# One change in four places of a fused attention and mixture-of-experts kernel: fp16 gate, early comparisons, other PSUM banks, another order on VectorE

## The chip, the cores and the metric

The kernel runs on one core of a Trainium2 chip. The metric is the device time of one execution in microseconds; the time before is the median of 3 runs. Engines: TensorE (PE for products, PEld for loading weights), VectorE (DVE), ScalarE (ACT), GpSimd (POOL) and SyncE (SP), which issues most transfers.

## The reference

Attention over 8 batches, 8 heads, 576 positions of 64, in two parts that are added: one on means of 4 positions, one local with |i - j| < 4. Its result, as 4608 tokens of 512, goes through a mixture of 8 experts of capacity 576. Pairs of token and expert are taken greedily in the order of their logits, so the routing follows the exact order of the logits.

```python
out_up = np.repeat(sm_attn(q_d, k_d, v_d), 4, axis=2)      # q_d: means of 4 positions
attn = softmax(np.where(abs(i - j) < 4, scale * q @ k.T, -1e9))
x = (out_up + attn @ v).transpose(0, 2, 1, 3).reshape(4608, 512)
logits = x @ w_gate                                        # 4608 x 8
for idx in np.argsort(-logits.flatten()):
    tok, e = idx // 8, idx % 8
    if assigned[tok] < 0 and counts[e] < 576:
        assigned[tok] = e; counts[e] += 1
for e in range(8):
    m = assigned == e
    out[m] = np.maximum(x[m] @ w1[e], 0) @ w2[e]           # 512 -> 1024 -> 512
```

## The kernel before, in words

**Attention** works on 36 units of 128 tokens. Each unit has stages (`LOC`): scores of 4 windows into the one PSUM tile `s` (`loc_s`), then maximum and difference on VectorE (L439, L440), exponential on ScalarE, transposes (`loc_t`), products with v (`loc_v`) and the normalising on VectorE (L397 to L400). Then `log_a` adds the other part of attention, `log_t` transposes the unit's 128 x 512 result and ScalarE scales it by XS into `xt` (fp32), and `log_m` multiplies it with the gate's weights `wgf` (fp32) into logits, which VectorE copies to `lg`. All but the scores use the 6 banks `g` in turn. The order is written out by hand: a list of works, sorted by a due time in units; `after(n, f)` puts a work n TensorE pieces later. Between the units stand the transposes and products of the other part of attention, batch by batch, so units lie at uneven distances. After unit 25 and after unit 35 a generator `setup` is stepped through: it makes 16-bit keys, high `xh` and low `xl`, out of the logits.

**Routing** takes one expert at a time (`phase`). Every token stands for its best open expert; a search on the high key and then on the low key finds the threshold at which the first expert fills. `count` does a search in levels: 64, 32 and 32 thresholds. On each level VectorE compares keys with thresholds (L687), TensorE counts by products (L717), VectorE subtracts (L725), sets a flag (L728), a product spreads it (L730), a reduction finds the level's answer (L732). In the first phase the first level's comparisons are made in `first_compare` into tiles `cmp0` of a pool that takes over the attention's memory, and counts below the first level take two token tiles to a product (`n = 2`), in the others four. `emit` ranks the chosen tokens and makes their list `idx`; `self.done` is its last operation. Then follow updates of the routing's state (`gl` to `used`, L914 to L931).

**Experts.** `gather` fetches an expert's 576 tokens by `idx` with 5 indirect transfers on GpSimd's queue. For the first two experts `piece` transposes them on TensorE into banks `pX` (2 of them), ScalarE writes the high fp16 half (L1057), VectorE the low one (L1058). For later experts a DMA transposes. `split` turns weights into fp16 halves, `wh` on ScalarE (L1026) and `wl` on VectorE (L1028). `mlp` computes products high x high, high x low, low x high: first 8 blocks of the hidden layer into banks `pH` (two tiles of 2 banks), whose result leaves as halves `ht` (ScalarE L1105, VectorE L1108), then 5 parts of tokens into `pX` (L1121). Each part is scaled by ScalarE and sent with an indirect transfer.

A scheduler orders the experts' part by priority; `high_priority` raises it, `issue_after(ins)` puts what is issued inside behind `ins` on the engine of `ins`, `behind_` does so for two instructions. `in1` is called after each hidden block and holds weight pieces (for the first expert, those of its own second product; later, those of the next expert); `in2` after each part of the second product, where the second expert's rows are transposed (`GET0`: pieces 0 and 1 after part 3, the others after part 4). `BEHIND` puts the second routing's rank products behind the first expert's second product, and `TURN` sets the place of the later transposes of the first expert's rows.

Of the kernel before, what the change touches and what calls it, by code (L numbers as in the profile page):

```python
# [6 lines left out]
F32 = mybir.dt.float32  # L7
F16 = mybir.dt.float16
# [82 lines left out]
class Attention:  # L91
    def __init__(self, ctx, tc, q, k, v, wg, ident, identb, maskc, x_dram, up_dram, lg, big, more=()):
# [20 lines left out]
        self.wgf = cst.tile([128, 4, E], F32, name="wgf")  # L113
        for t, src in ((self.ident, ident), (identh, identb), (self.mask, maskc)) + tuple(more):
            nc.scalar.dma_start(t, src)
# [17 lines left out]
    def gate(self):  # L133
        nc = self.nc
        nc.scalar.mul(self.wgf, self.wgf, GS)
# [349 lines left out]
    def log_t(self, u):  # L485
# [5 lines left out]
        xt = self.xt[u] = self.wk.tile([128, 4, 128], F32, name="xt", bufs=TB)  # L491
        nc.scalar.activation(xt.rearrange("p c t -> p (c t)"), p.rearrange("p c t -> p (c t)"), AF.Copy, scale=XS)

    def log_m(self, u):
        nc = self.nc
        xt = self.xt.pop(u)
# [138 lines left out]
class Routing:  # L635
    def __init__(self, ctx, tc, lg, consts):
# [22 lines left out]
        self.cuts = []  # L659
# [24 lines left out]
    def compare(self, cmp, key, thr, a, b):  # L684
        w = min(SW, thr.shape[1])
        r = thr.shape[1] // w
        self.nc.vector.tensor_tensor(cmp[:, a:b].rearrange("p t (r j) -> p t r j", r=r),  # L687
                                     key[:, a:b, None, :w].to_broadcast([128, b - a, r, w]),
                                     thr.rearrange("p (r j) -> p r j", r=r)[:, None].to_broadcast([128, b - a, r, w]),
                                     op=OP.is_ge)  # L690

# [4 lines left out]
    def first_compare(self, key, cut):  # L696
        cmp = self.wk.tile([128, NT, LV[0][0]], BF, name="cmp0", bufs=2)
        for a, b in cut:
            self.compare(cmp, key, self.first, a, b)
        return cmp  # L700

    def count(self, oh, key, cmp, cap, full=None):
# [4 lines left out]
        for lv, (J, step) in enumerate(LV):  # L707
# [4 lines left out]
            n = 2 if self.cut is HALF else 128 // J  # L712
# [15 lines left out]
            nc.vector.tensor_tensor(fl[:J], cv[:J, :, 0], left[:J], op=OP.is_ge)  # L728
# [42 lines left out]
    def setup(self, a, b, first=False):  # L771
# [14 lines left out]
        if first:  # L786
            self.cuts += [(c, min(c + 18, b)) for c in range(a, b, 18)]
# [57 lines left out]
    def phase(self, last, first=False, known=None):  # L845
# [20 lines left out]
        if first:  # L866
            xh = self.v["xh"]
            early = self.first_compare(xh, self.cuts)
# [6 lines left out]
        if not first:  # L875
            early = self.first_compare(xh, WHOLE)
        H = self.count(oh, xh, early, lambda: self.cap)
        cmp0 = self.first_compare(xl, self.cut)
# [405 lines left out]
```

## Time and profile before

| | |
|---|---|
| median of 3 runs | 776.08 us (773.46 to 778.11) |
| profiled execution | 776.02 us, span 774.4 us |
| mean granted clock of TensorE | 0.941 |
| busy: TensorE, its loads, VectorE, ScalarE, GpSimd | 698.9, 498.9, 509.3, 331.1, 242.0 us |
| DMA | 124.98 MB, mean 161 GB/s |

The profile is that of one execution. Busy times overlap; a share of the span is a mean over stages with different limits. A clock of 1.00 is 2.4 GHz, one of 0.50 is 1.2 GHz. Rows of a time line are start, length, engine, line, operation, tiles and count; brackets hold the engine's idle time before the row and what ended it.

### The profile page before, as it was taken

What the parts mean: (1) busy time and instruction counts of PE and PEld (TensorE: products, weight loads), DVE (VectorE), ACT (ScalarE), POOL (GpSimd) and SP (SyncE); (2) the same over time, 40 slices, a digit from 0 to 9 for tenths busy, and PEclk for the clock granted to TensorE, in tenths of its full rate; (3) what the DMA queues carried; (4) which work ended last, traced back from release to release, by engine and by line L of the source; (5) the groups of instructions that cost most, each with busy time, mean ns of one, the idle gap of its engine ahead of it and who ended that gap; (6) DMA issues with size and microseconds to landing.
All of it is one profiled execution on the core that took longest, in us unless ns stands there. A gap on an engine that the chain in (4) does not pass through costs nothing.

```text
span 774.4 us, 20987 instructions
## 1 busy us (share of the span) xinstructions
PE 698.9 (90%) x8513; PEld 498.9 (64%) x8513; DVE 509.3 (66%) x1530; ACT 331.1 (43%) x635; POOL 242.0 (31%) x289
## 2 busy tenths in 40 slices
PE   7798999998999993589999999999999999999994
PEld 4677788887888893356466456356456465574752
DVE  5766576765676736877878989899979345271210
ACT  4546567673767430342523426135225244252210
POOL 4756264534537340300530413150230402201011
PEclk9789799997999985689999999999999999999998
DMA  9988889897988750522614566471673884605001
GB/s 261 215 230 212 236 225 256 235 231 237 240 206 216 177 165 11 185 95 91 210 41 147 171 145 219 90 279 36 191 211 109 118 283 95 199 1 102 22 28 34
DMA packets 148048, 124.98 MB, mean 161 GB/s; under 512 B 92144, under 2 KB 122352, under 8 KB 147952
## 3 DMA queue, kind: packets, MB, share of 16 engines
q1 hardware_dynamic: 140656, 102.12, 49.0%
q0 software_dynamic: 6432, 20.98, 9.0%
q8 instruction: 67, 1.10, 0.6%
q10 hardware_dynamic: 864, 0.55, 0.3%
q14 instruction: 29, 0.24, 0.1%
HBM read 95.30 MB, written 21.23 MB: 150 GB/s over the span
## 4 chain that ended last, share of the span: by engine, by line
PE 38%; issue 23%; DVE 23%; ACT 6%; DMA 4%; POOL 3%; SPq 1%; POOLq 0%; DVEq 0%; ACTq 0%
PE pH L1082 7%; DVE wl L1028 5%; PE g L499 4%; PE pX L1121 4%; PE g L472 4%; DMA nat<-in_k_dram 3%; PE g L289 3%; DVE cmp L687 3%; POOL out_dram L1130 2%; DVE ht L1108 2%; PE s L430 2%; PE g L450 2%; PE g L490 2%; PE g L366 2%; ACT pt L461 2%
## 5 line engine op out<-in xcount | busy, mean ns | idle before, releaser
L1082 PE MATMUL pH<-xt,wh 128*128 128x256 f16 (+1 forms) x1024 | 196.1, 288 | 7.8 <-DVE ht L1108 3.5
L1121 PE MATMUL pX<-wh,ht 128*128 128x512 f16 (+1 forms) x640 | 179.7, 384 | 2.3 <-DVE xt L1058 2.3
L1121 PEld LDWEIGHTS <-ht 128*128 128x128 f16 (+1 forms) x960 | 84.0, 101 | 100.6 <-issue 11.6
L1082 PE MATMUL pH<-xt,wl 128*128 128x320 f16 (+1 forms) x512 | 147.5, 288 | 0.0
L1130 POOL DMA_INDIRECT out_dram<-y,idx x40 | 47.3, 1181 | 248.6 <-ACT y L1127 226.6
L1082 PEld LDWEIGHTS <-wh 128*128 128x128 f16 x1024 | 98.7, 98 | 35.3 <-issue 7.3
L1121 PE MATMUL pX<-wl,ht 128*128 128x512 f16 (+1 forms) x320 | 119.2, 384 | 0.0
L1105 ACT ACTIVATE ht<-pH 128x512 f16<-128x512 f32 (+1 forms) x128 | 45.5, 408 | 128.7 <-PE pH L1082 128.7
L1028 DVE SCALAR_TENSOR_TENSOR wl<-nat,wh 128x512 f16<-128x512 f32 x128 | 84.8, 686 | 7.6 <-ACT wh L1026 5.2
L1127 ACT ACTIVATE y<-pX 128x512 f32<-128x512 f32 (+1 forms) x40 | 23.8, 594 | 130.9 <-PE pX L1121 83.5
L1108 DVE SCALAR_TENSOR_TENSOR ht<-pH,ht 128x512 f16<-128x512 f32 (+1 forms) x128 | 52.6, 451 | 34.1 <-ACT ht L1105 33.1
L1026 ACT ACTIVATE wh<-nat 128x1024 f16<-128x1024 f32 x64 | 66.8, 1057 | 4.7 <-DMA nat<-in_moe_w_dram 4.4
L1043 POOL DMA_INDIRECT xg<-x_dram,idx x40 | 47.8, 1195 | 57.7 <-DVE xs L1065 24.8
L1082 PEld LDWEIGHTS <-wl 128*128 128x128 f16 x512 | 50.3, 98 | 15.4 <-issue 3.2
L461 ACT COPY pt<-g 64x512 f32<-64x512 f32 x72 | 41.7, 579 | 37.1 <-PE g L450 35.9
L472 PE MATMUL g<-vw,pt 128*64 128x65 f32 x1152 | 45.2, 232 | 3.8 <-ACT pt L461 2.4
L262 POOL TENSOR_TENSOR gtmp<-kt 128x576 f32<-128x576 f32 x14 | 16.4, 1171 | 101.8 <-ACT kt L275 57.2
L472 PEld LDWEIGHTS g<-vw,pt 128*64 128x64 f32 x1152 | 40.3, 146 | 12.0 <-ACT pt L461 6.9
L289 PE MATMUL g<-ident,nat 128*128 128x128 f32 x256 | 41.3, 289 | 7.3 <-DMA nat<-in_k_dram 3.7
L1129 DVE SCALAR_TENSOR_TENSOR y<-pX,y 64x512 f32<-64x512 f32 x8 | 5.5, 693 | 61.6 <-ACT y L1127 61.6
L275 ACT COPY qt<-g 64x512 f32<-64x512 f32 (+1 forms) x50 | 31.1, 623 | 33.4 <-PE g L289 18.7
L275 ACT COPY kt<-g 64x512 f32<-64x512 f32 (+1 forms) x60 | 37.8, 630 | 13.9 <-PE g L289 13.0
(198 smaller groups left out, 1172.6 us busy)
## 6 DMA issues: line engine op xcount, KB each, us to landing
nat<-in_moe_w_dram SPq DMA_DIRECT2D x28, 1024.0 KB
vw<-in_v_dram SPq DMA_DIRECT2D x136, 96.0 KB
up<-up_dram SPq DMA_DIRECT2D x36, 256.0 KB
x_dram<-x SPq DMA_DIRECT2D x36, 256.0 KB
nat<-in_q_dram SPq DMA_DIRECT2D x16, 512.0 KB
nat<-in_k_dram SPq DMA_DIRECT2D x16, 512.0 KB
nat<-in_v_dram SPq DMA_DIRECT2D x14, 512.0 KB
up_dram<-xu SPq DMA_DIRECT2D x16, 128.0 KB
```

The lines of the kernel that those rows point to most:

```text
L275: self.nc.scalar.copy(out, in_)
L289: nc.tensor.transpose(p[:, a, :, fp], src[:, 4 * hh + 2 * a + s, 2 * fp:2 * fp + 2].rearrange("p f d -> p (f d)"), self.ident)
L461: self.nc.scalar.copy(out, in_)
L472: nc.tensor.matmul(o[64 * i:64 * i + 64, 65 * h:65 * h + 65], pt[:, 2 * (h % 2) + i, 2 * g + h // 2].rearrange("p b q -> p (b q)"), self.v ...
L1026: nc.scalar.activation(hi, r, AF.Copy, scale=sc)
L1028: nc.vector.scalar_tensor_tensor(lo[:, a:a + LOP], r[:, a:a + LOP], sc, hi[:, a:a + LOP], op0=OP.mult, op1=OP.subtract)
L1043: self.fetched = nc.gpsimd.indirect_dma_start(out=xg[:n], out_offset=None, in_=self.x, in_offset=bass.IndirectOffsetOnAxis(ap=idx[:n, c:c ...
L1082: mm = nc.tensor.matmul(p[:, s, :s1 - s0], w[d][a][:, 128 * f:128 * f + 128], xt[:, b, d, s0:s1], start=j == 0, stop=j == len(seq) - 1)
L1105: last = nc.scalar.activation(hi, q, AF.Relu)
L1108: nc.vector.scalar_tensor_tensor(lo, q, 0.0, hi, op0=OP.max, op1=OP.subtract)
L1121: mm = nc.tensor.matmul(p[o:o + m], ht[:, f, h0:h0 + m], w[4 + f // 2][b][:, 512 * (f % 2):512 * (f % 2) + 512], start=j < parts, stop=j > ...
L1130: i = nc.gpsimd.indirect_dma_start(out=self.out, in_=y[:n], in_offset=None, out_offset=bass.IndirectOffsetOnAxis(ap=idx[:n, c:c + 1], axis=0))
```

## The change

Four parts. The gate's input and weights become pairs of fp16 halves, made on ScalarE (high) and VectorE (low); four fp32 products become four fp16 ones of 16 columns and four of 8, and a reduction adds the two halves' sums. The first level's comparisons of both keys go into `setup`, into two tiles `level` of their own that are there from the start; the low key's last tiles are compared in `count`, behind the first flag (`beside`), and lower levels of the first phase count four tiles to a product. The second expert's rows 0 to 3 are transposed into pairs of banks `pH`. On VectorE the state's updates and the second routing stand behind the second low half of the first expert's tokens (`lows[NXT]`), and pieces in `in1` behind the low half of `ht`.

```diff
     def gate(self):
-        nc.scalar.mul(self.wgf, self.wgf, GS)
+        nc.scalar.activation(self.wg16[:, :, 0], self.wgf, AF.Copy, scale=GS)
+        nc.vector.scalar_tensor_tensor(self.wg16[:, :, 1], self.wgf, GS, self.wg16[:, :, 0],
+                                       op0=OP.mult, op1=OP.subtract)
...
-        xt = self.xt[u] = self.wk.tile([128, 4, 128], F32, name="xt", bufs=TB)
-        nc.scalar.activation(xt.rearrange("p c t -> p (c t)"), p.rearrange("p c t -> p (c t)"), AF.Copy, scale=XS)
+        xt = self.wk.tile([128, 2, 4, 128], F16, name="xt", bufs=TB)
+        pf = p.rearrange("p c t -> p (c t)")
+        hi = xt[:, 0].rearrange("p c t -> p (c t)")
+        nc.scalar.activation(hi, pf, AF.Copy, scale=XS)
+        self.after(FT, lambda: nc.vector.scalar_tensor_tensor(xt[:, 1].rearrange("p c t -> p (c t)"), pf, XS, hi,
+                                                              op0=OP.mult, op1=OP.subtract), ("x", u))
...
-        l = self.ps.tile([128, E], F32, name="g", bufs=NG)
+        l = self.ps.tile([128, 2, E], F32, name="g", bufs=NG)
         for c in range(4):
-            nc.tensor.matmul(l, xt[:, c], self.wgf[:, c], start=c == 0, stop=c == 3)
-        nc.vector.tensor_copy(self.lg[:, u], l)
+            nc.tensor.matmul(l, xt[:, 0, c], self.wg16[:, c].rearrange("p s e -> p (s e)"),
+                             start=c == 0, stop=False, skip_group_check=True)
+        for c in range(4):
+            nc.tensor.matmul(l[:, 0], xt[:, 1, c], self.wg16[:, c, 0], start=False, stop=c == 3,
+                             skip_group_check=True)
+        nc.vector.tensor_reduce(self.lg[:, u], l.rearrange("p s e -> p e s"), axis=AX.X, op=OP.add)
...
+    def compares(self, i, a, b):
+        for c in range(a, b, 18):
+            self.compare(self.level[i], self.v[("xh", "xl")[i]], self.first, c, min(c + 18, b))
+            yield
...
-            n = 2 if self.cut is HALF else 128 // J
+            n = 128 // J
...
+            if beside and lv == 0:
+                with self.tc.issue_after(last.ins):
+                    beside()
...
+        if first:
+            yield from self.compares(0, a, b)
...
+        if first and b < NT:
+            yield from self.compares(1, a, b)
+        self.rest = a
...
-            p = self.ps.tile([128, 4, 128], F32, name="pX", bufs=2)
+            if first or c == 4:
+                p = self.ps.tile([128, 4, 128], F32, name="pX", bufs=2)
+            else:
+                if c % 2 == 0:
+                    pair[c // 2] = self.ps.tile([128, 2, 512], F32, name="pH", bufs=2)
+                p = pair[c // 2][:, c % 2].rearrange("p (d s) -> p d s", d=4)
...
                 for lo, q, hi in los:
-                    nc.vector.scalar_tensor_tensor(lo, q, 0.0, hi, op0=OP.max, op1=OP.subtract)
-            in1(f, last)
+                    low = nc.vector.scalar_tensor_tensor(lo, q, 0.0, hi, op0=OP.max, op1=OP.subtract)
+            with self.tc.issue_after(low.ins):
+                in1(f, last)
...
+                ro.behind_(ro.left, ex.lows[NXT])
...
-                    with tc.high_priority(), tc.issue_after(ro.done.ins) if i == 1 else nullcontext():
+                    with tc.high_priority(), tc.issue_after(ex.lows[NXT].ins if i == 0 else ro.done.ins) if i < 2 else nullcontext():
```

## Rows read from the trace of the kernel before

**Rows 1.** Busy time by stretch: length, PE, PEld, DVE, ACT, POOL, clock, DMA share, GB/s
```profile
80.00:284.00 204.00, 192.07 (x3966) 171.39 (x3966) 137.56 (x402) 126.87 (x254) 96.14 (x125) 0.96 0.87 228
284.00:292.00 8.00, 7.86 (x39) 7.76 (x37) 0.50 (x3) 1.19 (x2) 0.03 (x1) 0.50 0.04 16
292.00:318.00 26.00, 9.32 (x137) 7.66 (x138) 18.39 (x78) 2.47 (x4) 0.18 (x2) 0.50 0.16 54
...
326.00:394.00 68.00, 60.16 (x438) 37.19 (x438) 53.31 (x159) 25.10 (x47) 17.84 (x12) 0.92 0.36 128
394.00:452.00 58.00, 55.84 (x480) 33.26 (x478) 50.96 (x171) 21.67 (x41) 10.64 (x11) 1.00 0.43 130
...
670.00:717.00 47.00, 47.00 (x314) 29.37 (x312) 20.76 (x38) 18.80 (x34) 4.78 (x5) 1.00 0.24 51
```

**Rows 2.** Groups of instructions by form: count, busy us, mean ns, idle before
```profile
L717 PEld LDWEIGHTS <-cmp 128*128 128x128 bf16 x468 | 15.1, 97 | 16.7 <-DVE cmp L687 10.3 <-DVE ol L882 2.8 <-issue 2.6
L1058 DVE SCALAR_TENSOR_TENSOR xt<-pX,xt 128x512 f16<-128x512 f32 x8 | 5.4, 684 | 1.3 <-ACT xt L1057 1.3
```

**Rows 3.** Time line of TensorE: end of attention, and one count at full clock
```profile
280.02 1.06 PE L499 MATMUL g<-wgf,xt 128*128 128x8 f32 x8
280.93 0.64 PE L490 MATMUL g<-ident,x 128*128 128x128 f32 x4
...
286.73 5.13 PE L499 MATMUL g<-wgf,xt 128*128 128x8 f32 x24
...
349.92 0.60 PE L717 MATMUL pR<-ol,cmp 128*128 128x16 bf16 x18
```

**Rows 4.** Busy time of four short stretches, columns as in rows 1
```profile
120.00:130.00 10.00, 9.18 (x169) 7.63 (x168) 5.29 (x15) 9.78 (x23) 0.80 (x2) 1.00 1.12 279
140.00:150.00 10.00, 10.00 (x262) 9.09 (x258) 7.93 (x27) 4.71 (x10) 9.24 (x13) 1.00 0.70 203
...
342.00:346.00 4.00, 4.00 (x29) 2.59 (x28) 1.47 (x7) 0.00 (x0) 0.00 (x0) 0.62 0.02 4
...
390.00:394.00 4.00, 4.00 (x25) 2.23 (x22) 2.53 (x5) 0.47 (x1) 3.08 (x2) 0.64 0.25 93
```

**Rows 5.** Time line of VectorE and GpSimd: copies of logits, first routing
```profile
81.34 0.16 DVE L500 COPY lg<-g 128x8 f32<-128x8 f32 x1
...
277.12 0.16 DVE L500 COPY lg<-g 128x8 f32<-128x8 f32 x1
...
281.51 1.27 POOL L480 TENSOR_TENSOR x<-x,up 128x512 f32<-128x512 f32 x1 [0.65 <-DVE lg L500]
...
293.80 0.16 DVE L500 COPY lg<-g 128x8 f32<-128x8 f32 x1
...
296.74 0.69 DVE L687 TENSOR_TENSOR cmp<-xl,first 128x1024 bf16<-128x1024 int16 x1
```

**Rows 6.** Time line of TensorE, VectorE and ScalarE in the first expert
```profile
318.81 0.24 DVE L914 TENSOR_SCALAR gl<-kx,val 128x36 bf16<-128x36 f32 x1
...
325.43 0.60 ACT L1057 ACTIVATE xt<-pX 128x512 f16<-128x512 f32 x1 [0.92 <-PE pX L1053]
...
326.74 1.27 DVE L1058 SCALAR_TENSOR_TENSOR xt<-pX,xt 128x512 f16<-128x512 f32 x2
...
328.06 0.37 PE L1082 MATMUL pH<-xt,wh 128*128 128x256 f16 x1 [1.60 <-DVE xt L1058]
...
337.61 0.68 DVE L1108 SCALAR_TENSOR_TENSOR ht<-pH,ht 128x512 f16<-128x512 f32 x1
...
341.50 0.49 PE L1082 MATMUL pH<-xt,wh 128*128 128x256 f16 x2 [3.21 <-DVE ht L1108]
...
363.27 0.30 DVE L763 TENSOR_TENSOR_SCAN sumf<-one,f 128x72 bf16<-128x72 bf16 x1
...
370.06 0.20 PE L766 MATMUL pR<-f,tri 128*128 128x72 bf16 x1
...
388.98 0.38 PE L1121 MATMUL pX<-wh,ht 128*64 128x512 f16 x1 [2.33 <-DVE xt L1058]
```

More of the change, by code (lines that the diff above doesn't have):

```diff
@@ L113, in __init__ @@
         self.wgf = cst.tile([128, 4, E], F32, name="wgf")
+        self.wg16 = cst.tile([128, 4, 2, E], F16, name="wg16")
         for t, src in ((self.ident, ident), (identh, identb), (self.mask, maskc)) + tuple(more):
@@ L658, in __init__ @@
         self.v = {}
-        self.cuts = []
+        self.level = [st.tile([128, NT, LV[0][0]], BF, name=f"level{i}") for i in range(2)]
         self.behind = None
@@ L694, in behind_, with first_compare, count @@
             mybir.DependencyClass.NoSync, mybir.DependencyReason.DATA), reason="behind")
[L696 to L702, printed above, removed]
+    def first_compare(self, i, key):
+        self.compare(self.level[i], key, self.first, 0, NT)
+        return self.level[i]
+    def count(self, oh, key, cmp, cap, full=None, beside=None):
         nc, wk = self.nc, self.wk
@@ L727, in count @@
             fl = wk.tile([128, E], BF, name="fl")
-            nc.vector.tensor_tensor(fl[:J], cv[:J, :, 0], left[:J], op=OP.is_ge)
+            last = nc.vector.tensor_tensor(fl[:J], cv[:J, :, 0], left[:J], op=OP.is_ge)
+            if beside and lv == 0:
+                with self.tc.issue_after(last.ins):
+                    beside()
             njp = self.ps.tile([128, E], F32, name="pR", bufs=2)
@@ L786, in setup @@
         if first:
-            self.cuts += [(c, min(c + 18, b)) for c in range(a, b, 18)]
             lm = self.lg[:, a:b].rearrange("p t e -> p e t")
@@ L867, in phase @@
             xh = self.v["xh"]
-            early = self.first_compare(xh, self.cuts)
+            early = self.level[0]
         else:
@@ L875, in phase @@
         if not first:
-            early = self.first_compare(xh, WHOLE)
-        H = self.count(oh, xh, early, lambda: self.cap)
-        cmp0 = self.first_compare(xl, self.cut)
+            early = self.first_compare(0, xh)
+        if first:
+            cmp0 = self.level[1]
+            H = self.count(oh, xh, early, lambda: self.cap, None, lambda: self.compare(cmp0, xl, self.first, self.rest, NT))
+        else:
+            H = self.count(oh, xh, early, lambda: self.cap)
+            cmp0 = self.first_compare(1, xl)
         e = t("e")
@@ L982, in __init__ @@
         self.ident = ident
-        self.sc, self.second, self.sent, self.products, self.turns = [], {}, None, [], []
+        self.sc, self.second, self.sent, self.products, self.turns, self.lows = [], {}, None, [], [], []
     def weights(self, ei, late):
@@ L1032, in split, with gather @@
         return w, piece
-    def gather(self, idx, first):
+    def gather(self, idx, first, second=False):
         nc = self.nc
@@ L1068, in piece_dma @@
                                             xs[:n].rearrange("p a d -> p (a d)"))
-        return xt, piece if first else piece_dma
+        return xt, piece if first or second else piece_dma
     def mlp(self, w, xt, idx, in1, in2, first=False):
@@ L1145 @@
 TURN = (6, 12, 18)
+NXT = 1
 SPIN = 24
```

12 lines of the change are left out of this document (8 added, 4 removed).

## The prediction, made blind

> **What bounds the kernel now.** I read the stretches by stage first [rows 1]. From 80 to 284 us (attention and gate) TensorE is busy 192.1 of 204.0 us at a clock of 0.96, so TensorE sets the pace there; but VectorE has 137.6, ScalarE 126.9 and the DMA share is 0.87, so no engine is far off. From 284 to 292 only the last gate products run, at the lower of the two clock levels (0.50, which is 1.2 GHz). From 292 to 318 TensorE is busy 9.3 of 26.0 us: the first expert is being routed, and the chain runs over VectorE. The first expert then takes 68 us, the second 58, the seventh 47, and in that one TensorE is busy all the time: 47 us is the price of an expert's products alone, so about 21 us of the first and 11 of the second are routing work and stalls. Second I read the time line around each place that the diff touches: the gate [rows 2, 3], two short stretches of attention [rows 4], the end of attention and the first routing [rows 5], the first expert's stalls [rows 6]. What counts there is the wait in brackets in front of a TensorE row, and the clock after it.
>
> **The fp16 gate, steady part.** Removed per token tile: four fp32 products, 8 records, 0.91 us of TensorE (from 280.02 to the next row at 280.93) [rows 3]. Added: eight fp16 products of 16 or 8 columns. The nearest row is the counting of the routing, 18 load-and-product pairs of 16 columns in 0.60 us at full clock, 33 ns each [rows 3]: 8 x 33 ns = 0.27 us. TensorE saves 0.64 us per tile. A bound from the other side is the load's own record, 97 ns [rows 2]: 8 x 97 ns = 0.78 us, a saving of 0.13 us. I take the pace, since pairs follow one another here too. The Trainium skill, "TensorE: Matmul & The Clock Gate", section "LDWEIGHTS (loading the stationary operand)", gives a load as its columns over 1.2 in ns, so 107 ns for 128 columns; 8 in a row would be an estimate of 0.85 us, and the gate would then gain 0.06 us a tile. The trace agrees with it for one load (97 ns), but 18 pairs in 0.60 us show that loads here overlap the products in front of them.
>
> VectorE gets one low half per tile, 512 columns out of PSUM: 0.68 us from the same operation on the experts' rows [rows 2]. The reduction that replaces the copy of the logits is a read of 16 columns in place of 8; I cost it at nothing beyond 0.02 us, within what the copy (0.16 us) takes now. ScalarE writes fp16 where it wrote fp32, at 0.60 us by the experts' same operation [rows 6]; no change. The first two keys' comparisons of tiles 0 to 25 also move into attention: four instructions; at 0.69 us for 16 tiles [rows 5] an estimate of 0.69 x 26 / 16 = 1.1 us for each key, inside VectorE's idle time there. If VectorE had none, these 2.2 us would show in full.
>
> How much of 0.64 us is kept? 29 of the 36 gate copies lie between 81.34 and 277.12 us [rows 5] (the first and the last of them). Of their 28 gaps 14 are under 5.2 us and 14 longer. In a stretch of short gaps TensorE is busy 10.00 of 10, but VectorE 7.93 of 10 [rows 4]; with two and a half tiles in it VectorE would get 1.7 us more, 9.6 of 10. There VectorE takes over as the bound, and I take no gain. In a stretch of long gaps VectorE has room (5.29) but ScalarE has 9.78 of 10 [rows 4]. I take two thirds of 14 x 0.64 = 9.0, that is 6 us. Bounds: 29 x 0.64 = 18.6 us gained, or nothing, or a loss (rivals).
>
> **The end of attention.** Seven tiles' gate products stand behind the last scores, from 280.02 to 291.86 us: three at full clock, one across, and the last 24 records in 5.13 us (1.71 us a tile) [rows 3]. With fp16 they no longer set the end; the last tile's chain does. Its add on GpSimd ends at 281.51 + 1.27 = 282.78 us [rows 5]; then transposes 0.64 [rows 3], high half 0.60, low half 0.68 [rows 2], products at half clock 0.53, reduction 0.16: about 285.5 us with handing over. Before, the last copy of logits started at 293.80 [rows 5], some 1.9 us after the last product, since comparisons of the first key that needed attention's memory stood ahead of it on VectorE. Those now lie in attention. Together -8.3 us, with bounds from -5 (a TensorE that waits for the low halves of seven tiles, 7 x 0.68 = 4.8 in place of 11.9, less the 2 us) to -8.3.
>
> **The first routing.** The second key's comparison of 0.69 us sits between the first count and the row that uses it [rows 5]; it goes, and a shorter one (10 tiles, 0.43 us by that row) goes behind the first flag, where the product that the flag feeds covers part of it. I count 0.2 us for it, so -0.5 us (bounds -0.7 and -0.3). The four finer counts of this phase use 9 products in place of 18, and two more subtractions each: 9 x 66 ns at half clock, 0.6 us less, against two short VectorE operations of at least 0.16 us [rows 5] with their handing over. I take zero; bounds -0.3 and +0.2 each, so -1.2 to +0.8.
>
> **The first expert.** Ten updates of routing state (the first takes 0.24 us at 318.81 [rows 6]; an estimate of 2.3 us in all) and the first step of the second routing stand ahead of the low halves of tokens now. The second high half is ready at 325.43 + 0.60 = 326.03, the two low halves run from 326.74 to 328.01, and TensorE waits to 328.06 [rows 6]. With the updates behind them the second low half ends at about 326.7: -1.3 us. Queued behind the waiting update is all of the second routing, so it starts later than now, by the 2.3 us less what the low halves gain, about 1 us.
>
> At 337.61 the low half of the first hidden block starts, but weight pieces run between it and its 64-column rest, and TensorE waits 3.21 us to 341.50 [rows 6]. With pieces behind the low halves, the bank is free at about 338.4: -3.1 us, and the four us after it need no longer run at 0.62 [rows 4]: -1.5 us. What is late next is the pieces, by the 0.2 us of the 64-column rest, and they are needed only for the second half of this expert.
>
> The rows of the second expert are turned in the pX banks, so the last part of the first expert waits 2.33 us, to 388.98, for a low half to leave one [rows 6], and 390 to 394 runs at 0.64 [rows 4]. In pH banks: -2.3 and -1.4 us. The next user of pH is the second expert's first product, which needs the same low halves anyway.
>
> Sum 1.3 + 3.1 + 1.5 + 2.3 + 1.4 = 9.6 us. Against it: the second routing's mask is scanned at 363.27 and TensorE takes it at 370.06 [rows 6], 6.8 us of lead; TensorE comes up to 5.9 us earlier and the routing starts 1 us later, so the lead is used up and some of it may show. I give back 1.6 us and take -8. Bounds: 0 to -9.6. For later experts the pieces' place is that of now (low halves already go first), so I cost it at nothing; the cover is TensorE's own stream, and if it goes, VectorE (51.0 of 58 us in the second expert [rows 1]) is late by one piece a block, 0.68 us by the like operation [rows 2].
>
> **Sum.** -6 - 8.3 - 0.5 - 8 = -22.8 us. The profiled execution took 776.02 us with a span of 774.4; the median of the runs is 776.08. 776.0 - 22.8 = 753 us.
>
> **Rivals.**
> - *TensorE stays the bound through attention:* all 29 tiles keep 0.64 us, 12.6 us more: 740 us. For it: 10.00 of 10 busy [rows 4]. Against: VectorE's 7.93 in the same stretch.
> - *Attention's steady part gains nothing*, since loads (DMA share 0.87, and 1.12 in a stretch [rows 1, 4]), ScalarE and VectorE hold the pace: 759 us.
> - *Loads do not overlap:* fp16 records cost 97 ns each, 0.13 us a tile is saved; steady about -1, the end 0.5 us less: 759 us. That is the rule of the skill's page on loads, above; by 18 pairs in 0.60 us it has little chance.
> - *The experts give it back:* the second routing becomes what TensorE waits for, or the second expert, where VectorE is already 88% busy [rows 1], absorbs it: 8 us less gain, 761 us.
> - *Other side:* the low half stands in front of the scores' reduction on VectorE, which frees the single bank of scores, so TensorE waits in every tile. 29 x 0.68 = 19.7 us lost and the 6 not gained: 779 us; and each wait that pulls the clock down costs 1.5 us more, as after 341.50. It decides from about 0.8 us per tile on, where it eats the other 17 us and the 6.
> - *It does not do what it says:* the gate's end is bound elsewhere and the stalls move rather than go: 774 us.
>
> **How the numbers follow.** Forecast 0.50 (its own range 746 to 760); TensorE-bound 0.14; steady nothing 0.13; loads 0.04; given back 0.10; other side 0.06; nothing 0.03. Leaving out the last two and a little at the low end, the range is 739 to 767. No change means within 0.5%, 772 to 780 us, about what a measurement of this kernel can tell. The first five cases are faster: 0.91. The last two split into 0.05 same and 0.04 slower.
>
> **What would show it.** The gate's eight products take 0.3 us at full clock; the short-gap stretches keep their length with VectorE above 9 of 10, the long ones lose half a us a tile; the last logits come some 8 us less after the last scores; no wait for a low half of ht at the third block; the last part of the first expert follows its transposes at once, and 390 to 394 has the full clock. Wrong would be: TensorE waiting for the scores' bank in attention, or for the second routing's mask near its rank products.

## The result, and the profile after

After: 764.7 us (median of 4 runs, 763.87 to 766.96). Before, beside it: 777.1 us (4 runs, 773.46 to 778.98). The ratio is 0.9851, with an interval of 0.9807 to 0.9894: 11.6 us faster by the ratio (8.2 to 15.0), where the prediction had 22.8. The sign and the range held; the sum was twice too large. The profiled execution after took 764.85 us, span 763.2. Where a kernel ran several times, medians and ratios, here and below, leave out the executions that took over 1.5% longer than its fastest.

Busy time of the kernel after in the stretches of [rows 1] and [rows 4], moved by what the routing came earlier where they lie behind it (columns as there):

```profile
80.00:284.00 204.00, 171.16 (x3959) 148.91 (x3959) 156.76 (x446) 127.37 (x254) 94.83 (x124) 0.97 0.88 226
284.00:292.00 8.00, 2.00 (x26) 1.30 (x26) 6.18 (x32) 0.65 (x2) 0.00 (x0) 0.50 0.11 27
292.00:318.00 26.00, 12.87 (x105) 8.98 (x106) 20.25 (x73) 6.26 (x7) 7.72 (x8) 0.63 0.44 132
316.00:384.00 68.00, 63.71 (x501) 39.81 (x500) 57.67 (x178) 27.66 (x51) 16.89 (x12) 0.95 0.38 131
384.00:442.00 58.00, 54.94 (x462) 32.51 (x462) 48.86 (x171) 20.25 (x37) 11.61 (x11) 1.00 0.45 134
378.00:382.00 4.00, 2.32 (x22) 1.43 (x20) 2.74 (x8) 0.60 (x1) 0.32 (x1) 0.88 0.23 67
```

The first line holds the surprise. TensorE is busy 171.2 us where it was 192.1 [rows 1], 21 us less, in a stretch that holds almost the same work: it became idle, not shorter. The DMA share (0.88) and the rate (226 GB/s) are those of before. The second line is the gate's old end: TensorE busy 2.0 us in place of 7.9, and VectorE is already routing. The last line stands for 390 to 394 before [rows 4]: the granted clock is 0.88 there in place of 0.64.

The end of attention and of the first expert's rows, time line of three engines in the kernel after:

```profile
278.16 0.25 PE L508 MATMUL g<-wg,xt 128*128 128x16 f16 x4
278.26 0.24 PE L511 MATMUL g<-wg,xt 128*128 128x8 f16 x4
278.36 0.64 PE L493 MATMUL g<-ident,x 128*128 128x128 f32 x4
...
279.41 1.27 POOL L483 TENSOR_TENSOR x<-x,up 128x512 f32<-128x512 f32 x1 [2.10 <-DVE lg L513]
...
282.81 0.27 PE L511 MATMUL g<-wg,xt 128*128 128x8 f16 x4 [0.45 <-DVE xt L498]
...
283.12 0.17 DVE L513 TENSOR_REDUCE lg<-g 128x8 f32<-128x16 f32 x1 [0.28 <-PE g L511]
...
315.20 0.69 DVE L1092 SCALAR_TENSOR_TENSOR xt<-pX,xt 128x512 f16<-128x512 f32 x1 [0.96 <-ACT xt L1091]
315.81 0.23 DVE L941 TENSOR_SCALAR gl<-kx,val 128x36 bf16<-128x36 f32 x1
...
324.66 0.82 DVE L1142 SCALAR_TENSOR_TENSOR ht<-pH,ht 128x512 f16<-128x512 f32 x2
...
373.19 0.66 PE L1087 MATMUL pH<-ident,xg 128*128 128x128 f32 x4 [1.62 <-DVE xt L1092]
...
379.53 0.30 PE L1116 MATMUL pH<-xt,wh 128*128 128x320 f16 x1 [1.36 <-ACT xt L1091]
```

A unit's eight fp16 products take 0.20 us (278.16 to 278.36; 0.91 before [rows 3]). The last logits follow the last add on GpSimd by way of one unit's chain. The closing updates (`gl`) stand behind the second low half, and both low halves of `ht` are one row of 0.82 us, with no wait of TensorE in front of the third block. These are the steps as predicted. The last two rows are new waits, on `pH` and on the second expert's rows.

The next table is read from the time lines of all profiles: the end of the last value product (the steady part of the attention ends there), from there to the start of the last logits, on to the first gather (L1070 after), from the first expert's first gather to the second's and to the third's, and from the sixth's to the seventh's (us). Each line is one execution; kernels with the same chip number ran on the same chip. e11_dma2 is left out here; its numbers stand in the text.

| kernel | chip | last value product | to last logits | to first gather | 1st to 2nd | 1st to 3rd | 6th to 7th |
|---|---|---|---|---|---|---|---|
| before | - | 280.1 | 13.7 | 25.9 | 58.9 | 113.4 | 45.2 |
| c2_before | 11 | 280.4 | 12.1 | 25.8 | 58.7 | 113.1 | 45.2 |
| c4_before | 5 | 276.0 | 13.3 | 25.9 | 58.7 | 113.2 | 45.2 |
| after | - | 277.5 | 5.6 | 24.8 | 54.8 | 109.3 | 50.7 |
| c3_after | 12 | 277.5 | 5.6 | 24.8 | 54.3 | 106.9 | 51.0 |
| e1_pad20 | 7 | 278.6 | 5.5 | 24.8 | 53.9 | 107.7 | 50.8 |
| e1_pad64 | 7 | 280.1 | 5.2 | 24.8 | 56.1 | 108.9 | 50.9 |
| e2_gate32 | 7 | 276.4 | 10.8 | 24.8 | 54.1 | 108.0 | 51.9 |
| e3_nolow | 7 | 273.9 | 4.4 | 24.8 | 56.2 | 108.8 | 51.0 |
| e9_gateonly | 12 | 278.8 | 9.0 | 25.9 | 58.7 | 111.7 | 51.0 |
| e4_pair | 11 | 282.8 | 6.0 | 24.8 | 54.3 | 106.7 | 45.2 |
| e6_pX | 11 | 280.3 | 5.2 | 24.8 | 53.6 | 107.8 | 45.2 |
| e7_in1 | 11 | 278.7 | 5.6 | 24.8 | 54.2 | 106.3 | 45.2 |
| e8_both | 12 | 277.0 | 5.6 | 24.8 | 53.3 | 107.5 | 51.8 |
| e14_edge | 5 | 283.0 | 5.6 | 24.8 | 53.9 | 106.0 | 45.2 |
| e16_noedges | 10 | 276.4 | 5.2 | 24.8 | 58.6 | 111.2 | 51.6 |
| e10_pe3 | 5 | 279.9 | 6.5 | 24.8 | 52.8 | 106.0 | 45.2 |
| e15_store2 | 5 | 294.6 | 8.6 | 24.8 | 53.8 | 111.8 | 45.2 |
| e17_half_up | 10 | 268.0 | 5.6 | 24.8 | 53.3 | 111.8 | 51.9 |

The first column of times scatters by up to 7 us from one execution to the next (276.0 to 283.0 where nothing but the gate differs in that stretch), so one profile of each kernel says little there. The next two hardly scatter. From the first to the second gather the kernels with the experts of after show 52.8 to 56.2, all below the 58.7 to 58.9 of before; to the third they scatter by 5.8 us (106.0 to 111.8). The last column has two values, 45.2 and 50.7 to 51.9, which the profile of after against that of before made look like a loss of 5.5 us by the change.

### The profile page after: what moved, and what is told of

The parts are those of the page before. It is cut to its first block, busy times and chain, and to the rows that moved or that the text cites. A ratio compares the mean times of both kernels' runs of the same rounds, so it can differ in the third digit from the quotient of the medians.

```text
span 763.2 us, 20950 instructions
## 1 busy us (share of the span) xinstructions
PE 667.4 (87%) x8477; PEld 465.2 (61%) x8477; DVE 529.9 (69%) x1576; ACT 331.6 (43%) x635; POOL 241.3 (32%) x289
## 5 line engine op out<-in xcount | busy, mean ns | idle before, releaser
L1162 ACT ACTIVATE y<-pX 128x512 f32<-128x512 f32 (+1 forms) x40 | 23.8, 595 | 122.7 <-PE pX L1156 79.0
L1070 POOL DMA_INDIRECT xg<-x_dram,idx x40 | 49.3, 1233 | 60.1 <-DVE xs L1099 24.6
L1164 DVE SCALAR_TENSOR_TENSOR y<-pX,y 64x512 f32<-64x512 f32 x8 | 5.5, 693 | 58.9 <-ACT y L1162 58.8
```

The lines of the kernel that those rows point to most:

```text
L1070: self.fetched = nc.gpsimd.indirect_dma_start(out=xg[:n], out_offset=None, in_=self.x, in_offset=bass.IndirectOffsetOnAxis(ap=idx[:n, c:c ...
```

## The experiments

The theory at the start: the steady part gained little since TensorE was not what set its pace; the first expert gained half since waits moved to the pH banks; and the change brought a new wait in the sixth phase. The rivals: TensorE's idle time in the attention is VectorE's low halves at work; the pH banks are worth what they were priced at; the wait of the sixth phase has nothing to do with the change.

**The standstill of the sixth phase.** TensorE and VectorE of the kernel after, time line:

```profile
545.90 0.76 DVE L700 TENSOR_TENSOR cmp<-xh,thr 128x1152 bf16<-128x1152 int16 x1
...
546.71 0.39 PE L733 MATMUL pR<-oh,cmp 128*128 128x32 bf16 x9 [0.23 <-issue]
...
551.19 0.16 DVE L741 TENSOR_TENSOR less<-cap,pR 32x8 f32<-32x8 f32 x1 [4.54 <-remote]
...
551.98 0.16 PE L749 MATMUL pR<-fl,one 32*128 32x8 bf16 x1 [3.79 <-DVE fl L744]
```

The nine counting products are through by 547.1, as the profile models their ends, and the subtraction that reads them begins at 551.19; the wait's releaser is nothing that the profile knows ("remote"). The first two runs move all later instructions of VectorE by 20 and 64 places.

```diff
         nc.vector.memset(self.wm, 1.0)
+        none = cst.tile([128, 1], F32, name="none")
+        for _ in range(20):                  # e1_pad64: 64
+            nc.vector.memset(none, 0.0)
```

> The changed kernel with 20 VectorE fills of one column more at the very start, where VectorE waits for the first loads; nothing else moves. Theory A (place in VectorE's instruction stream): the 4.5 us for which VectorE stands at 546.7 us, in the fourth expert, belongs to an instruction's place in the stream. 20 instructions, at some 3 per us there, put that place about 7 us earlier; the wait is gone or stands elsewhere, and the time is about 760 us. Rival B (VectorE waits there for data): the wait stays in front of the same subtraction, 764 to 766 us.

> As the run before with 64 fills. Theory A: the place moves by about 21 us in that expert, the wait in front of the subtraction is gone, 759 to 762 us unless another place is met that costs as much. Rival B: the same wait at the same subtraction, 764 to 767 us.

Measured: 765.0 us (ratio to before 0.9902, 0.9848 to 0.9955) and 767.5 (0.9889, 0.9848 to 0.9931). The wait of 4.6 us stands at the same subtraction in both. So it does not hang on a place in the stream of instructions.

Kernels before and after, unchanged, profiled again:

> The kernel before, unchanged, profiled once more on the chip that runs the other kernels of this call. It tells whether the 4.5 us in which TensorE and VectorE both stand still in the middle of the sixth routing phase (551 us after, in every variant so far, nowhere in the one profile of before) belong to the change. Theory A (they belong to what the change does to the order or the place of the work): the stretch from the first gather of the sixth set of rows to that of the seventh takes 45.2 us again, with no wait over 1.5 us of a VectorE less for the counts. Theory B (they belong to the chip or the execution, not to the kernel): a wait of 4 to 5 us shows here too, and the stretch takes 50 us. The first gather of the second set comes 58.9 us after that of the first, within 1 us, by both.

> The kernel after, unchanged, on the chip that runs the other kernels of this call. In the profile shown first, and in four variants on one chip, TensorE and VectorE stood still for 4.5 us in the sixth routing phase; three other variants on another chip did not. Theory A (it belongs to the chip or the execution): 45 us from the sixth to the seventh gather here, no wait over 1.5 us for the counts, and 760 us in all. Theory B (it belongs to the order that the change writes, and the three variants happen to undo it): 50 to 51 us again, 764 to 766 in all.

> The kernel before, unchanged, once more, beside the other kernels of this call. The 4.5 us standstill of the sixth routing phase stood in after on three chips and also in the kernel with the fp16 gate alone, whose experts are those of before; it was missing in three variants of after and in two profiles of before. Theory A (it goes with the chip): if the other kernels of this call show it, so does before, and its sixth set takes 50 us to the seventh gather; if they do not, before does not. Theory B (the order of the kernel before avoids it): 45.2 us here, whatever the others show.

Measured: c2_before 780.2 us (one execution), c3_after 765.0 (0.9844, 0.9786 to 0.9901), c4_before 770.2 (one). The standstill is in every kernel on chips 7, 10 and 12, also in e9_gateonly, whose experts' code is that of before; it is in no kernel on chips 5 and 11, among them six that have all or nearly all of the change. So it goes with the chip and not with the change. By themselves the three repeats would have misled: c2_before came out as its theory A (the change) has it, c3_after as its theory B (the order that the change writes), and c4_before fits both of its theories; the kernels beside them decide otherwise. The wait in c3_after:

```profile
549.19 0.16 DVE L741 TENSOR_TENSOR less<-cap,pR 32x8 f32<-32x8 f32 x1 [4.70 <-remote]
```

What it is stays open, and since each chip was used at one time only, the chip and the time are not told apart. The kernel before itself was never profiled on a chip that shows it; its run times lean the same way (medians 775.9 and 778.5 us on chips 7 and 12, 16 and 13 runs; 771.8 on chip 11, 7 runs), which does not prove it.

**The gate: its parts alone.**

e2_gate32 undoes the fp16 gate and keeps the rest; e9_gateonly has it alone; e3_nolow leaves the low half out:

```diff
 # e2_gate32 (after with the gate of before); e9_gateonly is the reverse, on before
-        xt = self.wk.tile([128, 2, 4, 128], F16, name="xt", bufs=TB)
+        xt = self.xt[u] = self.wk.tile([128, 4, 128], F32, name="xt", bufs=TB)
...
+            nc.tensor.matmul(l, xt[:, c], self.wgf[:, c], start=c == 0, stop=c == 3)
+        nc.vector.tensor_copy(self.lg[:, u], l)
 # e3_nolow
-        self.after(FT, lambda: nc.vector.scalar_tensor_tensor(xt[:, 1].rearrange("p c t -> p (c t)"), pf, XS, hi,
-                                                              op0=OP.mult, op1=OP.subtract), ("x", u))
...
-            nc.tensor.matmul(l[:, 0], xt[:, 1, c], self.wg16[:, c, 0], start=False, stop=c == 3,
+            nc.tensor.matmul(l[:, 0], xt[:, 0, c], self.wg16[:, c, 0], start=False, stop=c == 3,
```

> The changed kernel with the gate of the kernel before (fp32 products, no low half), all other parts kept. By the forecast's terms the fp16 gate is worth 6 us of steady attention and 6.4 us at its end, so +12 us: 777 us. By the two traces it is worth 2.5 and about 6.4 us: +9, 774 us. Theory A adds that 36 VectorE instructions fewer move the place of the 4.5 us wait, so that up to 5 us come back: 769 us.

> The changed kernel without the gate's low half on VectorE; the four products that read it read the high half, so TensorE's work is that of the changed kernel and VectorE has 0.68 us less per tile. Theory C (VectorE's low half is what holds attention's steady part): the last products with v, which end at 277.5 us, end 10 us earlier or more. Rival D (ScalarE's copies, loads and TensorE's own stream hold it): they end at 274 to 277 us, at most 3 us earlier.

> Before, with the fp16 gate alone: the products, the low halves, the reduction, nothing else of the change. Theory A (the prediction's: TensorE sets the pace of the attention): the last value product ends 6 us earlier than in before (274 for 280), the last logits come 6 to 8 us behind it in place of 13.7, and the program is 11 to 14 us shorter than before. Theory B (in the steady part nothing is gained, because another bound stands as near): the last value product ends at 278 to 282, the end gives 5 to 6 us, and the program is 4 to 7 us shorter than before.

Measured: e2_gate32 773.7 us (0.9989, 0.9943 to 1.0035), e3_nolow 762.4 (0.9863, 0.974 to 0.9986), e9_gateonly 772.0 (0.9952, 0.9914 to 0.9991). With the fp32 gate the value products end at 276.4 us, no later than with fp16; with fp16 alone at 278.8, within what before itself shows (276.0 to 280.4). So no gain of the steady part shows within that scatter (B of e9_gateonly). The end gains 3 to 5 us by fp16 alone (9.0 in place of 12.1 to 13.7) and 5.2 by fp16 on top of the rest (5.6 for 10.8); the rest of the change, which has the early comparisons, brings 2 to 3 there. The last logits of e9_gateonly, time line of VectorE, start without a wait for TensorE, behind the comparisons that the rest of the change moves into the attention:

```profile
286.05 1.09 DVE L700 TENSOR_TENSOR cmp<-xh,first 128x1152 bf16<-128x1152 int16 x2 [0.34 <-issue]
287.06 0.82 DVE L700 TENSOR_TENSOR cmp<-xl,first 128x1280 bf16<-128x1280 int16 x1
287.79 0.17 DVE L513 TENSOR_REDUCE lg<-g 128x8 f32<-128x16 f32 x1
```

Without the low half the value products ended 3.6 us earlier than in after, in one execution. That is neither of the two sizes written down for it (10 or more, 3 or less), and 2.1 us below the earliest end in any other kernel with all its transfers (276.0): whether VectorE's 36 rows of 683 ns cost the steady part anything is not shown, but it is far from their sum of 24.6 us. The groups of the gate in after, by form (count, busy us, mean ns, idle before):

```profile
L498 DVE SCALAR_TENSOR_TENSOR xt<-g,xt 128x512 f16<-128x512 f32 x36 | 24.6, 683 | 3.7 <-ACT xt L497 3.6
...
L508 PE MATMUL g<-wg,xt 128*128 128x16 f16 x144 | 9.1, 172 | 0.3 <-ACT xt L497 0.3
...
L511 PE MATMUL g<-wg,xt 128*128 128x8 f16 x144 | 8.7, 167 | 0.4 <-DVE xt L498 0.4
```

TensorE hardly waits for the two halves (0.3 and 0.4 us in all). In front of the scores, where the prediction's rival on the other side had put the loss, it stands once, for 2.6 us, in the list below (`s`).

**What sets the pace of the attention.** TensorE's longest waits between 80 and 280 us in after, by releaser (us in total, times, longest):

```profile
PE g L475 <- ACT pt L464: 4.7, 5, 1.3
PE g L292 <- ACT qt L278: 3.4, 4, 1.1
PE g L453 <- ACT sw L445: 3.2, 4, 1.4
PE g L453 <- ACT qt L278: 3.1, 3, 1.4
PE s L433 <- issue: 2.6, 1, 2.6
```

They are many and small, and they name ScalarE, which is busy 127 of 204 us. This list does not name the transfers, which the runs below show to count. Four runs multiply one cost each, or halve one.

```diff
 # e10_pe3
+        for _ in range(3):
             for c in range(4):
                 nc.tensor.matmul(l, xt[:, 0, c], self.wg16[:, c].rearrange("p s e -> p (s e)"),
                                  start=c == 0, stop=False, skip_group_check=True)
...
 # e15_store2 (a second tensor); e11_dma2 issues the first tensor's store twice
+        getattr(self.nc, STQ).dma_start(self.x_more[128 * u:128 * u + 128], self.x[u])
 # e17_half_up
+        if u % 2:
+            self.up[u] = self.up[u - 1]
+            return
```

> After, with each tile's eight gate products issued three times over (they add onto one another, so the logits come out three times as large): at 33 ns a pair 0.53 us of TensorE more for each of 36 tiles, 19 us in all, nearly what the fp16 gate took off. Theory A (TensorE sets the pace of the attention): the last value product ends 15 to 19 us later than in after (277.5), at 293 to 297. Theory B (the fp16 gate only made idle time, since the copies or the transfers set the pace): it ends at 277 to 283.

> After, with each tile's rows of x stored twice to the same place: 36 more stores of 256 KB, 9.4 MB, on the queue that stores them now; no engine computes more. Theory A (the transfers, at a share of 0.88 of the 16 engines and 226 GB/s between 80 and 284 us, are the bound that took TensorE's place): the last value product ends 15 to 40 us later than 277.5 (9.4 MB at 226 GB/s is 42 us, less what slack there is). Theory B (the pace is set by the engines' chain of copies and products): at most 4 us later.

> After, with each tile's rows of x stored a second time, to another tensor, so that no store waits for another: 9.4 MB more, 36 more issues on the queue that stores them. Theory A (the 16 DMA engines, at a share of 0.88, set the pace of the attention): the last value product ends 15 to 40 us later than 277.5. Theory B (they do not): at most 4 us later. In the run with both stores to the same rows it came 15.6 us later, but with the share fallen to 0.67, so that one spoke of waits between stores.

> After, with the coarse part of the attention (up) loaded for every second tile of tokens only; the odd tiles add that of the tile before, so their x is not the reference's. It takes 18 loads of 256 KB, 4.7 MB, off the same queue and adds nothing. Theory A (the transfers set the pace of the attention): the last value product ends 8 to 20 us earlier than 277.5 (4.7 MB at 226 GB/s is 21 us, less what TensorE's 171 busy us then allow). Theory B (the longer end with 9.4 MB more only shows that transfers can become the bound): at most 3 us earlier.

Measured, one execution each: 758.7, 871.3, 782.1 and 762.1 us. e11_dma2 told nothing on bandwidth: each second store waited for the first, and the first gather came at 412.6. (Its last value product ended at 369.3, 92 us later than in after; the 15.6 us in the text of e15_store2 is wrong.) The waits of SP's queue in e11_dma2 (us in total, times, longest):

```profile
SPq L487 <- DMA x_dram<-x: 139.5, 36, 6.7
```

The other three decide. Busy time from 80 to 284 us in c4_before:

```profile
80.00:284.00 204.00, 191.76 (x3977) 170.63 (x3974) 136.09 (x401) 128.05 (x255) 94.38 (x122) 0.97 0.86 227
```

in e10_pe3:

```profile
80.00:284.00 204.00, 182.03 (x4484) 160.07 (x4485) 158.69 (x439) 127.92 (x254) 94.90 (x124) 0.98 0.88 227
```

in e15_store2:

```profile
80.00:284.00 204.00, 170.80 (x3797) 146.47 (x3794) 143.29 (x402) 122.87 (x245) 87.99 (x116) 0.93 0.94 249
```

and in e17_half_up:

```profile
80.00:284.00 204.00, 171.32 (x4001) 148.36 (x4000) 165.30 (x480) 128.02 (x255) 95.84 (x123) 0.96 0.79 205
```

With three times the gate's products TensorE is busy 11 us more and the value products end at 279.9 us, in the middle of what the others show. With 9.4 MB more to store, and no engine's work added, they end at 294.6, 17 us later than in after, at a share of 0.94. With 4.7 MB less to load they end at 268.0, 9.5 us earlier, at 0.79, with the engines as busy as in after or busier. Both lie outside the scatter, so transfers set the pace of after, though not alone: at 226 GB/s the bytes are worth 42 and 21 us (an estimate), and each run moved the end by less than half of that. Before, the stretch is no longer, with 21 us more of TensorE's work in it, so they very likely set it there too; no run changed the transfers of before. Whether it is the 16 DMA engines or the one queue that issues these transfers in order, the runs do not tell apart: 249 GB/s shows that 226 was not the most the engines can move.

**The first expert.**

```diff
 # e4_pair: the transposes of both pieces of a pair, then both pieces' halves
-        def piece(c):
+        def turn(c, p):
...
+            elif c % 2 == 0:
+                both = self.ps.tile([128, 2, 512], F32, name="pH", bufs=2)
+                for i in range(2):
+                    turn(c + i, ps[i])
+                for i in range(2):
+                    leave(c + i, ps[i])
 # e6_pX: pX for all five pieces
-            if first or c == 4:
+            if True:
 # e7_in1; e8_both is e4_pair and e7_in1 together
-            with self.tc.issue_after(low.ins):
-                in1(f, last)
+            in1(f, last)
 # e14_edge; e16_noedges is e7_in1 and e14_edge together
-                ro.behind_(ro.left, ex.lows[NXT])
...
-                    with tc.high_priority(), tc.issue_after(ex.lows[NXT].ins if i == 0 else ro.done.ins) if i < 2 else nullcontext():
+                    with tc.high_priority(), tc.issue_after(ro.done.ins) if i == 1 else nullcontext():
```

> After, but the two pieces of a pH pair of the second expert's rows are turned one right behind the other and only then copied out, so that the second bank of the pair no longer waits for the first one's low half. Theory A (the waits of 1.62, 1.36 and 0.3 us on pH between 373 and 381 us are what ate the gain of the first expert): the first gather of the second set comes 51.5 to 53.0 us after that of the first (54.8 in after), and the program is 2 to 3 us shorter than after, 762. Theory B (the pace there is set by the copies out of PSUM and by the next products' own inputs, the waits only show where): 54.0 to 55.5 us, no change, 765. The 5 us of the sixth phase stay by both.

> After, with the pH banks for the second expert's rows undone: all five pieces use the single pX banks as before; everything else of the change stays. Theory A (the pH banks bring what they were priced at, 3 us of the first expert): the first gather of the second set comes 57 to 58 us after that of the first, and the program takes 767 to 768. Theory B (they only move the wait from pX to pH): 54.0 to 55.5 us, as after, and 764 to 765. Theory C (the standstill of the sixth phase comes with the pH pieces): the stretch from the sixth to the seventh gather falls from 50.7 to 45 us; by A and B alone it stays at 50 to 51.5.

> After, with the weights' pieces no longer held behind the low halves of ht (that edge undone for all experts; the rest of the change stays). Theory A (the edge brings the 3.1 us it was priced at in the first expert): 57 to 58 us from the first gather to the second set's, with a wait of some 3 us of TensorE for ht as in before. Theory B (the edge is worth nothing by itself, since the pieces come late for DMA anyway): 54 to 55.5 us. Theory C (the edge, which holds for all eight experts, is what put the standstill into the sixth phase by another order on VectorE): the stretch from the sixth to the seventh gather is 45 us instead of 50.7. If none of A and C, the whole stays at 764 to 766.

> After, with the pieces of a pH pair turned together and with the weights' pieces no longer held behind the low halves of ht: two edits that gave 54.2 and 54.2 us from the first to the second gather, and 52.5 and 52.1 from the second to the third (54.8 and 54.5 in after). Theory A (they mend different waits): 52 and 51 us for these two stretches, and 4 to 5 us less than after in all. Theory B (both only take the same slack, which the routing chain sets): 53.5 to 54.5 and 52 us, 2 to 3 us less than after.

> After, without the edges that put the first routing's closing updates and the second routing phase behind the second piece's low half on VectorE (as before, where nothing orders them). The pH banks and the edge of the weights' pieces were each undone alone and cost nothing. Theory A (this order is what shortens the first expert): 57 to 59 us from the first gather to the second set's (54.3 in after). Theory B (the early comparisons of the first keys are enough, or the edges replace one another): 53.5 to 55 us.

> After, with both orders on VectorE undone at once: the weights' pieces behind the low halves of ht, and the first routing's closing updates and the second phase behind the second piece's low half. Each undone alone left 54.2 and 53.9 us from the first gather to the second set's. Theory A (either of them is enough): now 57 to 59 us, with TensorE waiting some 3 us for ht again, as before. Theory B (neither matters; the early comparisons and the pH banks bring it): 53.5 to 55 us.

Measured: e4_pair 760.9 us (0.9774, 0.9643 to 0.9905), e6_pX 761.6 (0.9856, 0.9768 to 0.9944), e8_both 768.4 (0.9889, 0.9828 to 0.995; c3_after on that chip 765.0); e7_in1 757.0, e14_edge 764.2 and e16_noedges 765.2, one execution each. Each of the three parts can be undone alone and 53.6 to 54.2 us stay from the first to the second gather: theory B of e7_in1 and e14_edge, and nearest to B of e6_pX. e4_pair takes the wait of 1.62 us away and has 54.3 us there (54.8 in after, 54.3 in c3_after), not 51.5 to 53.0: theory B. But the waits on the banks lie behind the second gather (373.19 against 362.76 in after), so only the third can show them: 107.8 us after the first in e6_pX and 106.8 in e4_pair, both within the scatter of 106.0 to 111.8. In e4_pair TensorE stands for the gathered rows instead (time line):

```profile
381.14 0.43 PE L1081 MATMUL pX<-ident,xg 64*128 64x64 f32 x4 [2.19 <-DMA xg<-x_dram,idx]
```

e8_both has 53.3 and 54.2 us for its two stretches, neither of its theories as a whole, and takes longer than c3_after on its chip, so no version better than after is shown. With both orders undone the old 58.6 us are back, and with them the old wait (time line of TensorE in e16_noedges):

```profile
328.10 0.39 PE L1116 MATMUL pH<-xt,wh 128*128 128x256 f16 x2 [3.21 <-DVE ht L1142]
```

So either order is enough to take this wait away (A of e16_noedges; one execution). Of the wait for the rows' low half, 1.60 us before [rows 6], 1.07 us stay in e14_edge, and nothing over 0.6 in e7_in1. The banks exchange waits (time line of TensorE in e6_pX):

```profile
374.26 0.58 PE L1156 MATMUL pX<-wh,ht 128*64 128x512 f16 x1 [2.33 <-DVE xt L1092]
```

That is the wait of [rows 6], back in full with `pX`, while in after 1.62 and 1.36 us stand on `pH` and on the rows themselves.

## Why the prediction was right in sign and twice too large

**Steady part, forecast -6: the step that failed.** The prediction read 192.1 of 204 us busy [rows 1] as "TensorE sets the pace there" and asked only what VectorE and ScalarE would leave of the saving. The saving itself was larger than priced: 0.71 us a unit (0.91 to 0.20), for 0.64. But no gain of it shows: the last value product ends at 278.8 us on average in three profiles of before and at 279.2 in the eleven kernels that have the fp16 gate and no further edit to the attention's steady work, e9_gateonly and the two padded ones among them (276.4 to 283.0). e10_pe3 shows that TensorE's slack holds half of the saving (10.9 of 20.9 us put back leave no trace), e15_store2 and e17_half_up that transfers set the pace of after. The share of 0.87, and 1.12 in a stretch, stood in [rows 1] and [rows 4], and the rival that named it got 0.13: for this term it was the case that came true.

The Trainium skill's page "Perfetto Trace Analysis", section "Identifying the Most-Contended Engine", warns that the busy share of matmuls is no measure of how near TensorE is to its limit. The trace agrees: 171, 182 and 192 busy us of 204 went with the same pace. The same section advises against the DMA engines' occupancy as a measure; here a share of 0.87 was the right pointer, and 0.79 and 0.94 went with 9.5 us less and 17 more.

**End of attention, forecast -8.3: right.** From the last value product to the last logits 13.0 us on average before, 5.6 after: -7.5. The prediction's chain, 5.4 us behind the last value product, is the one that shows. The Trainium skill's rule on loads ("TensorE: Matmul & The Clock Gate", section "LDWEIGHTS (loading the stationary operand)": columns over 1.2, in ns) does not give the pace here: eight load-and-product pairs follow one another in 0.20 us, where one load's record alone is 97 ns [rows 2].

**First routing, forecast -0.5: right.** 25.85 us to 24.80, -1.05, inside the bounds, and the same in every kernel with the change's comparisons.

**First expert, forecast -8: mis-sized, at about -4.** The second gather comes 4.0 and 4.6 us earlier in after and c3_after, the third 4.2 on average (113.3 us behind the first in three profiles of before, 109.0 in the ten kernels with the experts of after). The three terms 1.3, 3.1 and 1.5 are found. Busy time from the first expert's first product to the second routing's rank products, before and then after (columns as in [rows 1]):

```profile
326.07:370.06 43.99, 38.95 (x314) 26.33 (x314) 32.02 (x108) 13.56 (x29) 1.81 (x3) 0.92 0.32 116
315.21:353.07 37.86, 37.22 (x315) 25.71 (x315) 32.19 (x113) 12.97 (x28) 1.97 (x3) 0.95 0.19 65
```

TensorE's idle time there falls from 5.0 to 0.6 us, which is the 1.3 and the 3.1, and the same products take 1.7 us less at the higher clock: 6.1 us for the 5.9 of the prediction. Each order was priced by itself, though, and either one brings the 3.1. Behind the rank products part of it is given back, as the prediction reckoned. VectorE and TensorE in after, time line:

```profile
352.65 0.28 DVE L782 TENSOR_TENSOR_SCAN sumf<-one,f 128x72 bf16<-128x72 bf16 x1
353.07 0.20 PE L785 MATMUL pR<-f,tri 128*128 128x72 bf16 x1
...
358.55 2.72 DVE L1055 SCALAR_TENSOR_TENSOR wl<-nat,wh 128x512 f16<-128x512 f32 x4 [1.75 <-ACT wh L1053]
359.28 0.77 PE L989 MATMUL pR<-r,ohl 128*64 128x72 bf16 x18
...
361.31 0.19 DVE L993 COPY odd<-pR 32x36 f32<-32x36 f32 x1
```

The 6.8 us of lead are used up, without a wait of TensorE, but the products of L989 end while VectorE is in weight pieces: from their start to the gather it is 3.5 us, for 2.3 before (3.1 to 3.7 in every kernel with the second order, 2.3 in e14_edge and e16_noedges without it). Another 0.9 lies in the first product, 7.3 us behind the first gather for 6.4, which scatters (6.3 to 8.8 over all kernels).

The step that failed here is the pH term, 2.3 and 1.4, at one sentence: the next user of pH "needs the same low halves anyway". The nearer user is the second piece of the same pair: it waits at 373.19 for the first one's low half. No gain is seen. From the rank products to the second expert's first product it is 23.8 us in all three profiles of before, 22.0 to 25.7 in the kernels with the pH banks and 24.9 in e6_pX, which has 2.33 us back and loses nothing by it. So the rival that the experts give it back came true in part: by the 1.2 us of VectorE's pieces and by waits that moved. What TensorE waits for behind the second gather does not set how soon the third comes, as far as the scatter lets one see; what does set it is open.

**The sum.** 0 - 7.5 - 1.05 - 4.2 (first to third gather, above) = about -13 us by the profiles of all kernels, with the scatter of the first and the last term in it; the runs give -11.6 (8.2 to 15.0) and, for c3_after, -12.1 (7.7 to 16.7). One thing does not add up: the gate alone times at -3.7 us and the rest of the change alone (e2_gate32) at -0.9, together less than the whole. The intervals are 3 to 4.5 us wide to each side, and e2_gate32's own profile was 4.6 us quicker than its median; the runs do not settle it.

## What to carry to other kernels

An engine that is busy nine tenths of a stretch is a candidate for its bound, not more: before pricing what it will save, ask what the stretch would do if that work were doubled, and look at the DMA share as at any engine. When several edits aim at one wait, price the wait once, since any of them may remove all of it, and a bank that is swapped takes its wait along to the next tile that shares it. A gap that shows only in the profile after is not yet the change's: profile the kernel before beside it on the same chip.

## What was not expected of the hardware

At one and the same instruction, chips 7, 10 and 12, each at the one time it was used, let TensorE and VectorE stand for 4.5 to 4.8 us, and chips 5 and 11 did not, whatever the kernel; on the former the stretch takes 50.7 to 51.9 us, on the latter 45.2 in every profile. And 8 fp16 load-and-product pairs take 0.20 us at full clock, 25 ns a pair, quicker than the 33 ns of [rows 3] from which they were priced.
